# A planner's estimate of when transfers land and when GpSimd's queue slots come free, in a fused attention and MLP kernel on one core

## The chip, the core and the metric

The kernel runs on one core of a Trainium2 chip. The core has five engines that each work through a list of instructions in order: TensorE (PE in the profile, with its weight loads shown apart as PEld), VectorE (DVE), ScalarE (ACT), GpSimd (POOL) and SyncE (SP). They wait for each other by semaphores. SP, ACT and POOL also issue transfers (DMAs) between HBM and SBUF. Times are microseconds on the device; the metric is the median of the runs.

## The reference

The first half is attention with a squared ReLU in place of the softmax; its result, laid out as tokens by model width, goes through a two-layer MLP with a squared ReLU.

```
# q, k, v: (8, 12, 448, 64) float32; w_in: (768, 2048); w_out: (2048, 768)
scores = (1 / sqrt(64)) * q @ k.transpose(0, 1, 3, 2)
attn   = maximum(scores, 0) ** 2 / 448
o      = attn @ v                                  # (8, 12, 448, 64)
x      = o.transpose(0, 2, 1, 3).reshape(3584, 768)
h      = x @ w_in
r      = maximum(h, 0)
out    = (r * r) @ w_out                           # (3584, 768) float32
```

## The kernel before

**Work.** A unit `n` is four heads of one batch: 3 units per batch, 24 in all, 7 rounds per unit. For a unit the kernel brings q and k in, turns them (by TensorE, L441 with the copy L444, for units 0 to 5; by a transposing transfer on SP, L457, from unit 6 on, after a cast on GpSimd, L421) and brings v in (L471, two transfers). For each round TensorE makes scores (L502) into one of two PSUM tiles `sp`; the ReLU goes to one of four tiles `rel`, on VectorE (L529) or ScalarE (L532); the square goes to one of eleven tiles `at`, on ScalarE (L536) or GpSimd (L538). The seven squares of a unit are multiplied by v in one burst (L567), copied to `xt` (L587, L589). The first batch is cut in two parts by columns (128 and 320 of 448), so that work can start before all has landed.

**The MLP.** The first product of a batch is L629 (for the first part of the first batch L678, turned back at L705), its square and mask are L618 on ScalarE and L613 on VectorE. The second product is L778 for the first tokens and else L843, where seven products stand for eight (a Strassen scheme): their inputs are sums on VectorE (L822, `comb`), differences of the weights (L804 on GpSimd, L807 on VectorE), and results are copied (L762, L764), closed (L855) and stored by SP (L724). `rest` (L744, GpSimd) packs the last 64 tokens of two batches.

**First transfers.** GpSimd issues q and k of units 1 to 5 (L387), v (L471), the four quarters of `w_in` (L476, called w_0 to w_3 here, 768 KB each as written) and the four of `w_out` (L481). Its queue has eight slots in a ring, each with its own semaphore: the ninth transfer waits until the first has landed. GpSimd waits for this in its instruction list, so all that stands behind waits too.

**What sets the order.** No engine's list is written out by hand. Every operation is given to a `Plan` with its possible engines, costs, inputs, buffers and a due time. `simulate` runs a list schedule: each engine takes the earliest-due operation that is ready (`pick`), and the order in which operations were taken is the order in which they are emitted. A transfer's end in it comes from `land`, which shares a rate of 400e3 bytes per us among queues that have something to move, and adds a constant. For GpSimd, `self.sent` holds the time at which each transfer's slot comes free, and `pick` gives it no transfer while eight are taken:

```
if len(alt) == 5 and eng == "POOL" and sum(x > now for x in self.sent) > 7:
    continue
```

Sixteen pairs of two thresholds (`PATIENCE`: how long TensorE may idle before a filler matmul, L988, is put in its list, in the first 45 us; `LEAD`: how far ScalarE must be booked before GpSimd takes a late square) are tried, each with up to six rounds of `land`, and the schedule that ends first in the plan is emitted. On the chip, engines only wait for data: the plan's times are gone, its orders stay. TensorE starts with 9 matmuls on zeros (L985).

Of the kernel before, what the change touches and what calls it, by code (L numbers as in the profile page):

```python
# [42 lines left out]
class Plan:  # L43
# [72 lines left out]
    def land(self):  # L116


        queues: dict = {}
        for op in sorted((op for op in self.ops if op.size), key=lambda op: op.start):  # L120
            queues.setdefault(op.engine, deque()).append([op.start + 1.3, op.size, op])
        now, idle = 0.0, set(queues)
        while queues:
            for name in idle & set(queues):
                if queues[name][0][0] <= now + 1e-9 and set(queues) - idle:
                    queues[name][0][0] = now + 2.3
                    idle.discard(name)
            live = [name for name in queues if queues[name][0][0] <= now + 1e-9]
            idle -= set(live)
            if not live:  # L130
                now = min(q[0][0] for q in queues.values())
                continue
            rate = 400e3 / len(live)
            step = min(queues[name][0][1] / rate for name in live)
            later = [q[0][0] - now for q in queues.values() if q[0][0] > now + 1e-9]
            step = min([step] + later)
            now += step
            for name in live:
                q = queues[name]
                q[0][1] -= rate * step  # L140
                if q[0][1] <= 1e-3:
                    op = q.popleft()[2]
                    self.landing[op.id] = now + (
                        1.4 if len(queues) > 1 or now > 12.0 else 0.9) + (
                        1.0 if q and q[0][2].size > op.size else 0.0)
                    if not q or q[0][0] > now + 1e-9:
                        idle.add(name)
            queues = {name: q for name, q in queues.items() if q}

    def simulate(self):  # L150
# [10 lines left out]
        while done < len(self.ops):  # L161
            if not events:
                raise RuntimeError("no operation can go on")
            now = heapq.heappop(events)
            while events and events[0] <= now + 1e-9:
                heapq.heappop(events)
            again = True
            while again:
                again = False
                for eng in ("PE", "ACT", "DVE", "POOL", "SP"):  # L170
                    if self.busy[eng] > now + 1e-9:
                        continue
                    got = None
                    if eng == "PE" and last is not None and last.glue is not None:
                        soon = self.soon(last.glue)
                        if now < soon <= now + 0.45:
                            heapq.heappush(events, soon)
                            continue
                        if soon <= now:
                            got = waiting.index((last.glue.due, last.glue.id, last.glue)), (  # L180
                                last.glue.alts[0])
                    got = got or self.pick(eng, now, waiting)
                    if got is None:
                        if eng == "PE" and now < self.fill_until:
                            idle = now if idle is None else idle
                            if now < idle + self.patience:
                                heapq.heappush(events, idle + self.patience + 1e-3)
                            else:
                                self.fill(now)
                                heapq.heappush(events, self.busy[eng])  # L190
                        continue
                    z, alt = got
                    op = waiting.pop(z)[2]
                    _, busy, took, emit, *rest = alt
                    begin = now
                    op.size = rest[0] if rest else 0
                    if eng == "PE":
                        last, idle = op, None
                        begin += self.SWITCH.get((mode, op.mode), 0.0)
                        mode = op.mode  # L200
                        if now < self.cold:
                            busy, took = busy * 1.6, took * 1.6
                    if len(rest) > 1 and self.busy["POOL"] > now:
                        wait = self.busy["POOL"] - now
                        busy, took = busy + wait, took + wait
                    op.engine, op.start = eng, begin
                    op.end = begin + took
                    self.busy[eng] = begin + busy
                    if op.size:
                        op.end = max(begin + 2.2 + op.size / 390e3, self.landing.get(op.id, 0.0))  # L210
                        if eng == "POOL":
                            self.sent += [op.end] * (2 if op.size == 458752 and took > 1.0 else 1)
                    if len(rest) > 1:
                        self.busy["POOL"] = max(self.busy["POOL"], self.busy[eng])
                    for b in op.bufs:
                        if b.tile is None:
                            slot = min(x for x in self.pools[b.pool] if x[0] <= now + 1e-9)
                            self.pools[b.pool].remove(slot)
                            b.tile, b.slot = slot[2], slot[1]
                    self.order.append(emit)  # L220
                    heapq.heappush(events, self.busy[eng])
                    seen = op.end + self.LAG[eng]
                    for b in op.bufs:
                        b.left -= 1
                        b.end = max(b.end, op.end + 0.07)
                        if not b.left:
                            self.pools[b.pool].append((b.end, b.slot, b.tile))
                            heapq.heappush(events, b.end)
                    for x in op.nexts:
                        x.wait -= 1  # L230
                        x.ready = max(x.ready, seen)
                        if not x.wait:
                            insort(waiting, (x.due, x.id, x))
                            heapq.heappush(events, x.ready)
                    done += 1
                    again = True
# [922 lines left out]
```

## Time and profile before

| | |
|---|---|
| median of 5 runs | 386.84 us (386.36 to 388.29) |
| the profiled execution | 388.29 us, the highest of the five; its span is 386.4 us, so 1.9 us lie around it |
| PE busy | 372.7 us, 96% of the span |
| ACT busy, DVE busy, POOL busy | 279.3, 265.4, 173.5 us |
| squares on ScalarE, whole rounds (L536) | 108, 952 ns each |
| squares on GpSimd, whole rounds (L538) | 39, 1683 ns each |
| filler matmuls (L988) | 24 |
| TensorE clock granted | 1.000 |

The span runs from the first to the last instruction. "Busy" leaves out waits; a busy PE of 96% says that what can be won on the other engines is won only where TensorE waits for them. A group's line gives source line, engine, operation, tile written and tiles read, count, busy time and mean, and then the idle time of the engine before it with what ended it.

### The profile page before, as it was taken

The numbers are of one execution on the slowest core, as the hardware profiler recorded it, in microseconds if no ns is written. First come the engines' busy times: TensorE is split into PE (matmuls) and PEld (weight loads), VectorE is DVE, ScalarE is ACT, GpSimd is POOL, SyncE is SP. The second block draws the span as 40 slices with busy tenths as digits, with TensorE's granted clock in tenths as the row PEclk, the third lists the DMA queues.
The fourth block names the chain that finished last, engine by engine and source line by source line (L and its number), as shares of the span: only waits on it lengthen the run. The fifth ranks groups of instructions, "written<-read, shape, count | busy, mean of one in ns | idle before, by whom it ended". The sixth has DMA issues, their size and how long they took to land.

```text
span 386.4 us, 8331 instructions
## 1 busy us (share of the span) xinstructions
PE 372.7 (96%) x3299; PEld 198.1 (51%) x3299; DVE 265.4 (69%) x386; ACT 279.3 (72%) x417; POOL 173.5 (45%) x171
## 2 busy tenths in 40 slices
PE   7788999999999999999899999999999999999995
PEld 3545665544555445544455455544455546555563
DVE  2776789776876678676996675676886676256731
ACT  4988999898867887689786787695986785244221
POOL 6986558297753764562434444542602431001000
PEclk9999999999999999999999999999999999999999
DMA  9999999987578755569577664773562002210243
GB/s 185 177 208 193 177 225 236 230 183 169 72 201 188 166 146 113 114 164 233 61 192 124 155 158 87 186 172 68 146 125 61 2 3 52 65 28 1 55 110 83
DMA packets 70215, 51.34 MB, mean 133 GB/s; under 512 B 36896, under 2 KB 70176, under 8 KB 70176
## 3 DMA queue, kind: packets, MB, share of 16 engines
q1 hardware_dynamic: 52384, 35.86, 38.8%
q0 software_dynamic: 16928, 14.09, 24.7%
q10 hardware_dynamic: 864, 0.85, 0.6%
q8 instruction: 26, 0.43, 0.5%
q14 instruction: 13, 0.11, 0.1%
HBM read 45.61 MB, written 11.01 MB: 147 GB/s over the span
## 4 chain that ended last, share of the span: by engine, by line
PE 83%; DMA 8%; POOL 3%; DVE 2%; ACT 2%; issue 1%; SPq 0%; POOLq 0%
PE mm L629 36%; PE mm L843 29%; PE sp L502 8%; PE mm L567 7%; DMA vs<-in_v_dram 4%; PE mm L778 2%; DMA g<-in_k_dram 2%; DMA qkt<-blk 2%; DVE comb L822 1%; POOL at L538 1%; POOL w L476 1%; POOL g L387 1%; DVE rel L529 1%; ACT g L618 1%; PE mm L441 0%
## 5 line engine op out<-in xcount | busy, mean ns | idle before, releaser
L629 PE MATMUL mm<-xt,w 128*128 128x448 f16 (+1 forms) x768 | 148.9, 347 | 0.0
L538 POOL TENSOR_TENSOR at<-rel 128x896 f16<-128x896 f32 (+1 forms) x48 | 76.9, 1605 | 94.3 <-ACT rel L532 62.6
L613 DVE SCALAR_TENSOR_TENSOR g<-mm,g 128x448 f16<-128x448 f32 (+1 forms) x128 | 76.6, 605 | 54.4 <-ACT g L618 54.3
L536 ACT ACTIVATE at<-rel 128x896 f16<-128x896 f32 (+1 forms) x120 | 109.1, 931 | 3.6 <-PE mm L567 2.4
L629 PEld LDWEIGHTS <-w 128*128 128x128 f16 x768 | 72.2, 98 | 70.6 <-issue 12.3
L529 DVE TENSOR_SCALAR rel<-sp 128x896 f32<-128x896 f32 (+2 forms) x87 | 91.4, 1054 | 20.9 <-PE sp L502 17.3
L618 ACT ACTIVATE g<-mm 128x448 f16<-128x448 f32 (+1 forms) x128 | 66.9, 529 | 39.3 <-PE mm L629 38.6
L532 ACT ACTIVATE rel<-sp 128x896 f32<-128x896 f32 (+2 forms) x87 | 77.1, 891 | 7.2 <-PE sp L502 6.2
L843 PEld LDWEIGHTS <-comb 128*128 128x128 f16 x416 | 39.5, 98 | 31.7 <-issue 3.2
L502 PE MATMUL sp<-qkt,qkt 64*64 64x448 f16 (+2 forms) x756 | 50.8, 338 | 1.8 <-DVE rel L529 0.9
L421 POOL CAST blk<-raw 128x896 f16<-128x896 f32 x36 | 37.2, 1043 | 32.7 <-issue 15.9
L762 ACT ACTIVATE part<-mm 128x384 f32<-128x384 f32 x41 | 20.1, 489 | 42.0 <-PE mm L843 39.4
L855 DVE SCALAR_TENSOR_TENSOR part<-mm,part 128x384 f32<-128x384 f32 x52 | 28.7, 554 | 23.1 <-ACT part L762 14.3
L843 PE MATMUL mm<-wt,comb 128*128 128x384 f16 x208 | 37.0, 327 | 1.5 <-DVE comb L822 1.4
L843 PE MATMUL mm<-w,comb 128*128 128x384 f16 x208 | 36.8, 327 | 0.0
L567 PE MATMUL mm<-at,vs 64*64 64x448 f16 (+1 forms) x672 | 35.5, 343 | 1.1 <-POOL at L538 1.1
L843 PEld LDWEIGHTS <-g 128*128 128x128 f16 x264 | 25.2, 98 | 18.7 <-issue 2.5
L471 POOL DMA_DIRECT2D vs<-in_v_dram x48 | 29.8, 630 | 5.7 <-DMA w<-in_moe_w_in_dram 3.1
L502 PEld LDWEIGHTS <-qkt 64*64 64x64 f16 x756 | 18.1, 105 | 27.8 <-issue 23.9
L744 POOL COPY rest<-g 128x1024 f16<-128x1024 f16 x8 | 9.8, 1228 | 49.0 <-DVE g L613 49.0
L843 PE MATMUL mm<-w,g 128*128 128x384 f16 x176 | 30.9, 327 | 0.0
L567 PEld LDWEIGHTS <-vs 64*64 64x64 f16 x756 | 22.3, 107 | 14.0 <-issue 4.0
(60 smaller groups left out, 214.7 us busy)
## 6 DMA issues: line engine op xcount, KB each, us to landing
out_dram<-part SPq DMA_DIRECT2D x108, 96.0 KB, 2.2
raw<-in_k_dram SPq DMA_DIRECT2D x18, 448.0 KB, 4.1
raw<-in_q_dram SPq DMA_DIRECT2D x18, 448.0 KB, 4.8
vs<-in_v_dram POOLq DMA_DIRECT2D x48, 112.0 KB, 4.4
w<-in_moe_w_in_dram POOLq DMA_DIRECT2D x4, 768.0 KB, 12.2
w<-in_moe_w_out_dram POOLq DMA_DIRECT2D x4, 768.0 KB, 13.3
g<-in_k_dram POOLq DMA_DIRECT2D x4, 224.0 KB, 11.7
g<-in_q_dram POOLq DMA_DIRECT2D x4, 224.0 KB, 10.6
```

The costliest lines, as they stand in the source:

```text
L421: return lambda: fn(blk.tile.rearrange("p t (f d) -> p f t d", f=2), tile_of().rearrange("p f (t d) -> p f t d", d=D))
L471: nc.gpsimd.dma_start(out=buf.tile[64 * r:64 * r + 64], in_=src[:, u, hs])
L502: nc.tensor.matmul(sp[64 * c:64 * c + 64, e, c0:c0 + w].rearrange("p (t c) -> p t c", c=TP), lhsT=kT[r, t, 64 * e:64 * e + 64], rhs=qT[r, ...
L529: dve(n, lambda: nc.vector.tensor_scalar(out=rel(), in0=sp.tile[:, :, 0:width], scalar1=0.0, scalar2=SK, op0=ALU.max, op1=ALU.mult)),
L532: act(n, lambda: nc.scalar.activation(out=rel(), in_=sp.tile[:, :, 0:width], func=AF.Relu, scale=SK))],
L536: act(n, lambda: nc.scalar.activation(out=dst(), in_=rel(), func=AF.Square)),
L538: lambda: nc.gpsimd.tensor_mul(dst(), rel(), rel()))],
L567: nc.tensor.matmul(banks[f].tile[64 * e:64 * e + 64, c0:c0 + w], lhsT=vs[r, e ^ c, t * D:(t + 1) * D], rhs=a[r, e, :], start=(t == 0), sto ...
L613: nc.vector.scalar_tensor_tensor(out=dst, in0=src, scalar=0.0, in1=dst, op0=ALU.is_gt, op1=ALU.mult)
L618: nc.scalar.activation(out=dst, in_=src, func=AF.Square)
L629: nc.tensor.matmul(bank.tile[:, c0:c0 + w], lhsT=w1[f // 4][:, m, f % 4 * P:(f % 4 + 1) * P], rhs=xts[b].tile[:, m, cols], start=(m == 0), ...
L843: nc.tensor.matmul(buf.tile[:, 0:HALF], lhsT=lhs()[:, j, :], rhs=w[:, j, :], start=(first and j == 0), stop=(j == NH - 1), skip_group_chec ...
```

## The change

Three numbers in the plan change. In `land`, a transfer lands 2.1 us after its last byte has moved instead of 1.4 us (while more than one queue is at work, or after 12 us), and a transfer that is followed by a larger one in its queue gets 0.6 us more instead of 1.0 us. So a transfer is planned 0.7 us later, or 0.3 us later where a larger one follows. In `simulate`, a slot of GpSimd's ring comes free 0.8 us after the planned landing instead of at it. No operation, cost or buffer changes; the plan is made anew, and the emitted orders differ.

```
                     self.landing[op.id] = now + (
-                        1.4 if len(queues) > 1 or now > 12.0 else 0.9) + (
-                        1.0 if q and q[0][2].size > op.size else 0.0)
+                        2.1 if len(queues) > 1 or now > 12.0 else 0.9) + (
+                        0.6 if q and q[0][2].size > op.size else 0.0)
...
                         if eng == "POOL":
-                            self.sent += [op.end] * (2 if op.size == 458752 and took > 1.0 else 1)
+                            self.sent += [op.end + 0.8] * (2 if op.size == 458752 and took > 1.0 else 1)
```

The operations of the built program can be counted on each engine. After the change there are 36 filler matmuls instead of 24; 55 whole-round squares on GpSimd instead of 39, and 92 on ScalarE instead of 108; one of two pieces of a weight difference goes from GpSimd (L804) to VectorE (L807); four copies go from VectorE (L764) to ScalarE (L762); and some of the first copies and casts change between VectorE and ScalarE.

## The prediction

> **What bounds the kernel now.** I read the page's first lines, then the busy times by stage, then TensorE's waits by stage, then the timeline where a wait stands.
>
> ```profile
> PE 372.7 (96%) x3299; PEld 198.1 (51%) x3299; DVE 265.4 (69%) x386; ACT 279.3 (72%) x417; POOL 173.5 (45%) x171
> ```
> ```profile
> 0.00:32.00 32.00, 26.07 (x431) 14.90 (x432) 20.34 (x31) 25.22 (x38) 23.61 (x35) 1.00 1.12 191
> 32.00:45.00 13.00, 11.58 (x187) 7.48 (x185) 8.69 (x16) 11.24 (x18) 12.15 (x13) 1.00 1.16 176
> 45.00:350.00 305.00, 303.01 (x2494) 157.23 (x2493) 218.39 (x312) 234.20 (x346) 136.17 (x123) 1.00 0.62 133
> ```
>
> The second block has stage, length, busy PE, PEld, DVE, ACT, POOL, clock, DMA share, GB/s. From 45 to 350 us TensorE idles 1.99 us in 305; before 45 it idles 7.35 us, and some of its busy time there is filler. So the end is set by when TensorE gets its first data, then by its own work, then by a few waits. TensorE's waits from 45 to 350, then two of those before 45:
>
> ```profile
> PE mm L843 <- DVE comb L822: 1.2, 1, 1.2
> PE sp L502 <- DMA qkt<-blk: 0.6, 1, 0.6
> ```
> ```profile
> PE mm L567 <- POOL at L538: 1.1, 1, 1.1
> PE mm L678 <- DMA w<-in_moe_w_in_dram: 1.1, 2, 0.9
> ```
>
> After the last L678 both programs give TensorE the same matmuls, in the same order but for five places, with 122 changes between dense and 64x64 tiles instead of 124. So the difference is (a) when that L678 starts, (b) these waits, (c) new ones.
>
> **The start, to 32 us.** The timeline (start, length, engine, line; in brackets idle time before it):
>
> ```profile
> 11.07 0.84 POOL L476 DMA_DIRECT2D w<-in_moe_w_in_dram  x1 [0.68 <-DMA g<-in_k_dram]
> 11.93 1.26 POOL L538 TENSOR_TENSOR at<-rel 128x640 f16<-128x640 f32 x1
> 23.87 1.46 PE L678 MATMUL mm<-w,xt 128*128 128x512 f16 x6 [0.89 <-DMA w<-in_moe_w_in_dram]
> 31.97 0.59 POOL L471 DMA_DIRECT2D vs<-in_v_dram  x1 [3.10 <-DMA w<-in_moe_w_in_dram]
> 36.49 1.27 POOL L538 TENSOR_TENSOR at<-rel 128x640 f16<-128x640 f32 x1
> 37.82 0.47 PE L567 MATMUL mm<-at,vs 64*64 64x320 f16 x8 [1.09 <-POOL at L538]
> ```
>
> w_0 goes out at 11.07, when its slot is free, and the square follows. The landings of w_0 to w_3 in the trace are 20.02, 23.83, 27.66, 31.43: 3.8 us apart, one behind the other, and the four L678 start at 20.17, 23.87, 27.71 and 31.64. TensorE follows the weights. The DMA share is 1.29 at 12 to 13 us, 1.00 and 0.98 in the next two, 1.24 from 20: before w_0 the DMA engines ran partly dry, so w_0's landing hangs on its issue.
>
> The change puts that square ahead of w_0, and with w_0 all that GpSimd has behind it: the other weights, units 3 to 5, v. When can it run? Its rel is VectorE's second, read from the L502 that started at 9.14 behind turns which wait for k of unit 1 (landed 8.37). Seven fillers instead of one stand before the first turns: six more at 0.11 (six in a row take 0.83 in the trace, the last one's own 0.28 included) move them from 5.17 to 5.82. ScalarE then makes both copies, 256 and 512 columns, instead of VectorE: and one of the fillers waits for the first copy, since it writes the bank that is being read; the first scores start at about 7.1 instead of 6.95. All this ends in the wait for 8.37, which stays; behind it stands one more filler, 0.11. So rel is done at 10.45 instead of 10.34, the square runs 10.5 to 11.75, and w_0 goes out there: +0.7. A gain is excluded, for at 11.07 the slot had only just come free. Bounds: 0, if the dry stretch was the transfer's own and not its late issue; +1.35, if the 0.65 of the first turns gets through. I take +0.7, the row of the square. w_1 to w_3 are issued right behind (13.13 to 15.66 before, 12.6 to 15.1 now) and stay 3.8 us apart; their GpSimd waits cost nothing more. The last L678 starts at 32.3. The copies to xt, which the first L678 also needs, ended at 20.23 before; half a microsecond on them hides behind w_0's landing at 20.7.
>
> The other fillers (36 less 24, 1.3 us in all) stand where TensorE waits for w_1 to w_3, so the wait hides them; uncovered they cost 0.11 each.
>
> **32 to 45 us.** Before, GpSimd is stuck behind w_3's slot to 31.97, then does two squares (2.47), two transfers (35.0 to 36.5), then the square that TensorE waits for: at 37.82, 1.09 us of named wait and 1.4 us against the usual pace. After, only two squares are left behind the stuck v, one before each of the transfers of k and q: v at 32.7 to 33.3, square to 34.55, transfer to 35.3, square to 36.6. TensorE's burst starts 0.67 later, at 36.3, reaches the last two squares at 37.1, and does not wait. L441 follows at about 37.4 instead of 38.21; its second half needs q of unit 4, which landed at 37.19 and now lands near 37.9, so half a microsecond of gain is lost. What is late next is the copies to xt, which come with the burst. I take -0.65 at 45 us: +0.7 - 1.4 and a little; bounds -1.1 and +0.4.
>
> **78 us.** A turning transfer stands on SP behind four stores, is issued at 72.09 and lands at 77.95:
>
> ```profile
> 78.09 0.38 PE L502 MATMUL sp<-qkt,qkt 64*64 64x448 f16 x4 [0.63 <-DMA qkt<-blk]
> ```
>
> After, 12 of the L629 stand between this L502 and the one before it (at about 75.4). SP's list is the same up to here. TensorE arrives at about 78.2, when it has landed. 0.7 gained, 0.2 paid for two more changes of tile (a change back and forth takes 0.17 to 0.2 in the trace): -0.5, bounds -0.7 and 0.
>
> **186 to 189 us.**
>
> ```profile
> 185.49 2.60 POOL L421 CAST blk<-raw 128x896 f16<-128x896 f32 x2
> 187.23 1.41 DVE L822 TENSOR_TENSOR comb<-comb,g 128x1024 f16<-128x1024 f16 x1
> 188.69 1.47 PE L843 MATMUL mm<-wt,comb 128*128 128x384 f16 x8 [1.19 <-DVE comb L822]
> ```
>
> The sums of VectorE take 1.25 to 1.41 beside GpSimd's copies and casts, where undisturbed ones take 0.68. TensorE goes through two products at once and then waits for the second sum. After, an L502 pair (0.43) and a product without a sum (1.3) come between, 1.73 us of cover for 1.33 of wait (0.14 at 186.03, 1.19 here). I take -1.3; bounds -1.35 and 0, if GpSimd's three squares and its later rest copy hold VectorE up by as much again.
>
> **After that** the lists differ at 257 to 276 with four changes of tile fewer: -0.35 (bounds -0.4 and 0). The 16 squares moved take 15.2 us (16 x 0.952) from ScalarE and put 26.9 (16 x 1.683) on GpSimd; POOL is busy 136 of 305 there, so it has room, and ScalarE was no bound: 0 either way while the squares are done before their burst, which comes two pairs of L502, some 8 us, after the last scores. The end (last matmul, close, store) is the same list.
>
> **New waits.** Orders made with planned durations meet real ones. Before shows 2.0 us of such waits in three places after 45 us; for the new list I take a third, +0.7; bounds 0 and 4.
>
> For these last the nearest row is a square beside a sum:
>
> ```profile
> 240.54 1.68 POOL L538 TENSOR_TENSOR at<-rel 128x896 f16<-128x896 f32 x1 [1.19 <-ACT rel L532]
> 241.72 1.04 DVE L822 TENSOR_TENSOR comb<-comb,g 128x1024 f16<-128x1024 f16 x1
> ```
>
> The sum took 0.36 us more with 0.5 of the square left to run. The Trainium skill (SBUF — State Buffer, section "Who interferes with whom") speaks against the change here: a VectorE instruction with two SBUF inputs and a GpSimd one that reads SBUF block each other, the later waiting until the first is done. By that rule a sum that comes just behind a square's start loses up to the whole 1.68; three windows so hit would cost an estimated 3 x 1.68 = 5.0.
>
> **Sum.** -0.65 - 0.5 - 1.3 - 0.35 + 0.7 = -2.1. The span goes from 386.4 to 384.3. The profiled execution was the highest run (388.29); I put the same difference on the median, 386.84: 384.7.
>
> **Rivals.**
> *Given back* (0.20): the start costs the whole 1.35 instead of 0.7, and the sums of 188 us stay half as late; -2.1 + 0.65 + 0.65 = -0.8, so 386.0. For it: w_0 now waits for a chain of five engines' steps. Against: that chain meets at the landing of 8.37.
> *GpSimd in the way* (0.20): seven more windows like 186 us exist, where sums (L822) run; with more squares there, sums or the rest copy come late and TensorE waits 1.33 each. From the third window on it outweighs all: -2.8 + 3 x 1.33 = +1.2, so 388.0. For it: the rows above. Against: GpSimd would still be free for nearly half of the time (136 + 27 busy of 305), the long sums at 186 stand beside casts, whose number is unchanged, and beside a square a sum lost 0.36.
> *The orders differ but nothing that TensorE waits for does*: the three waits would have to stay; the lists at all three have changed. It is part of the first rival.
>
> **How the numbers follow.** 384.7 at 0.60. Without new waits and with the start at its better bound the sum is -2.8 - 0.45 = -3.25; the lowest run before lies 0.5 under its median, so the range begins at 383.1. The forecast's own range ends at 386.0, with new waits of 2.0. The whole range goes on over the first rival to 387.8, shortly before the second. About 0.3%, 1.2 us, is what a measurement of this kernel can tell from no change: the forecast lies beyond it on the fast side (0.60), the first rival within (0.20), the second beyond on the slow side (0.20).
>
> **What would show it.** Right: w_0 issued near 11.75 and landing near 20.7; the last L678 near 32.3; no wait of L567 for L538 near 37; no wait at L502 near 78; none at L843 near 186. Wrong: L678 past 33, or TensorE's idle time from 45 to 350 us above 3.

## The result, and the profile after

The changed kernel takes 385.52 us, median of 36 runs; the kernel before, run beside it, 387.42, median of 63. The ratio is 0.996 (95% interval 0.9948 to 0.9971), so the change makes it faster by 1.5 us (1.1 to 2.0) by the ratio and 1.9 by the medians. The prediction had a difference of -2.1 and 384.7; the kernel before came out 0.6 above the 386.84 that it was reckoned from.

The profiled execution took 385.16 us, its span is 383.4. That is 3.0 below the span before, more than the medians differ: the profile before was taken of a run 0.87 above the median of those 63, this one lies 0.36 below its own. The pair of profiles shows where time went; its total has 1.2 us of luck in it. One of the profiles further on (six fillers fewer) lies 6.6 us above its kernel's median; only its start and one wait are read.

The page of the changed kernel, then its busy times by stage (stage, length, busy PE, PEld, DVE, ACT, POOL, clock, DMA share, GB/s):

```profile
PE 374.7 (98%) x3311; PEld 200.5 (52%) x3311; DVE 267.5 (70%) x383; ACT 269.6 (70%) x407; POOL 194.3 (51%) x184
```
```profile
0.00:32.00 32.00, 28.62 (x442) 16.62 (x443) 20.45 (x32) 24.84 (x39) 22.97 (x33) 1.00 1.11 189
32.00:45.00 13.00, 12.70 (x194) 8.30 (x192) 10.01 (x17) 12.58 (x20) 11.04 (x13) 1.00 1.25 194
45.00:350.00 305.00, 304.39 (x2503) 158.64 (x2502) 220.60 (x310) 225.22 (x336) 158.76 (x138) 1.00 0.60 132
```

From 45 to 350 us TensorE idles 0.61 us (1.99 before). GpSimd is busy 22.6 us longer there, ScalarE 9.0 shorter, and VectorE 2.2 longer although it has two instructions fewer; the reason for the last number is given in the part on why the prediction was right. TensorE's waits, over the whole span (us in total, times, longest):

```profile
PE mm L678 <- DMA w<-in_moe_w_in_dram: 0.9, 1, 0.9
PE sp L502 <- DVE rel L529: 0.8, 3, 0.5
PE mm L567 <- ACT comb L536: 0.4, 2, 0.2
PE mm L843 <- DVE comb L822: 0.2, 1, 0.2
```

All three named waits of before are gone: L567 for L538 at 37 us, L502 for the transposing transfer at 78, L843 for a sum (1.2) at 188. A new one is in the second line. The timeline at the places that the prediction went through:

```profile
5.01 1.70 PE L988 MATMUL mm<-part 128*128 128x256 f16 x7
10.83 1.25 POOL L538 TENSOR_TENSOR at<-rel 128x640 f16<-128x640 f32 x1 [1.11 <-DVE rel L529]
12.03 3.36 POOL L476 DMA_DIRECT2D w<-in_moe_w_in_dram  x4
31.85 1.46 PE L678 MATMUL mm<-w,xt 128*128 128x512 f16 x6
36.10 1.15 PE L567 MATMUL mm<-at,vs 64*64 64x320 f16 x28
70.28 0.57 PE L502 MATMUL sp<-qkt,qkt 64*64 64x448 f16 x8 [0.48 <-DVE rel L529]
184.64 0.57 PE L502 MATMUL sp<-qkt,qkt 64*64 64x448 f16 x8
185.14 1.47 PE L843 MATMUL mm<-wt,g 128*128 128x384 f16 x8
185.29 2.33 DVE L822 TENSOR_TENSOR comb<-comb,g 128x1024 f16<-128x1024 f16 x1
186.45 2.76 PE L843 MATMUL mm<-wt,comb 128*128 128x384 f16 x16
```

The square is ahead of w_0, the burst (L567) runs through 28 matmuls without a stop, and at 185 us a pair of L502 and a product that reads no sum stand ahead of two products that run without a gap, although the second one's sum took 2.33 us. The starts of five matmuls that both programs have, and what each stage gained:

| start of | before | after | gain in the stage | predicted |
|---|---|---|---|---|
| the last L678 | 31.64 | 31.85 | +0.21 | +0.7 |
| the first L629 | 39.62 | 38.58 | -1.25 | -1.35 |
| the first L843 | 100.14 | 98.98 | -0.13 | -0.5, new waits +0.7 |
| the 400th L629 | 207.79 | 205.17 | -1.46 | -1.3 |
| the last matmul | 381.83 | 378.82 | -0.39 | -0.35 |

(The "400th" is that with 400 ahead of it, and so on.)

### The profile page after: what moved, and what is told of

It reads as the page before. It is cut to its first block, busy times and chain, and to the rows that moved or that the text cites. A ratio compares the mean times of both kernels' runs of the same rounds, so it can differ in the third digit from the quotient of the medians.

```text
span 383.4 us, 8363 instructions
## 1 busy us (share of the span) xinstructions
PE 374.7 (98%) x3311; PEld 200.5 (52%) x3311; DVE 267.5 (70%) x383; ACT 269.6 (70%) x407; POOL 194.3 (51%) x184
## 4 chain that ended last, share of the span: by engine, by line
PE 88%; DVE 5%; DMA 3%; ACT 2%; issue 1%; POOL 1%; DVEq 0%
PE mm L629 37%; PE mm L843 29%; PE sp L502 9%; PE mm L567 7%; DMA w<-in_moe_w_in_dram 3%; DVE comb L822 1%; DVE rel L529 1%; DVE wt L807 1%; PE mm L678 1%; PE mm L988 1%; PE mm L985 1%; ACT at L536 1%; PE mm L441 1%; PE mm L778 1%; ACT rel L532 0%
## 5 line engine op out<-in xcount | busy, mean ns | idle before, releaser
L629 PE MATMUL mm<-xt,w 128*128 128x448 f16 (+1 forms) x768 | 149.2, 347 | 0.0
L538 POOL TENSOR_TENSOR at<-rel 128x896 f16<-128x896 f32 (+1 forms) x63 | 102.4, 1626 | 90.2 <-ACT rel L532 57.9
L613 DVE SCALAR_TENSOR_TENSOR g<-mm,g 128x448 f16<-128x448 f32 (+1 forms) x128 | 76.5, 605 | 50.4 <-ACT g L618 50.2
L629 PEld LDWEIGHTS <-w 128*128 128x128 f16 x768 | 72.1, 98 | 70.2 <-issue 12.1
L529 DVE TENSOR_SCALAR rel<-sp 128x896 f32<-128x896 f32 (+3 forms) x87 | 90.7, 1046 | 22.4 <-PE sp L502 18.5
L536 ACT ACTIVATE at<-rel 128x896 f16<-128x896 f32 (+1 forms) x105 | 95.4, 926 | 4.8 <-PE mm L567 2.5
L618 ACT ACTIVATE g<-mm 128x448 f16<-128x448 f32 (+1 forms) x128 | 67.0, 529 | 45.0 <-PE mm L629 44.4
L532 ACT ACTIVATE rel<-sp 128x896 f32<-128x896 f32 (+1 forms) x87 | 77.6, 898 | 6.2 <-PE sp L502 5.1
L843 PEld LDWEIGHTS <-comb 128*128 128x128 f16 x416 | 39.8, 98 | 30.1 <-issue 3.5
L762 ACT ACTIVATE part<-mm 128x384 f32<-128x384 f32 x45 | 22.0, 488 | 44.0 <-PE mm L843 42.1
L502 PE MATMUL sp<-qkt,qkt 64*64 64x448 f16 (+2 forms) x756 | 51.2, 338 | 1.3 <-DVE rel L529 0.8
L421 POOL CAST blk<-raw 128x896 f16<-128x896 f32 x36 | 36.1, 1012 | 23.6 <-DMA raw<-in_k_dram 14.6
L843 PE MATMUL mm<-wt,comb 128*128 128x384 f16 x208 | 37.0, 327 | 0.2 <-DVE comb L822 0.2
L843 PE MATMUL mm<-w,comb 128*128 128x384 f16 x208 | 36.8, 327 | 0.1
L567 PE MATMUL mm<-at,vs 64*64 64x448 f16 (+1 forms) x672 | 35.3, 343 | 0.0
L843 PEld LDWEIGHTS <-g 128*128 128x128 f16 x264 | 25.2, 98 | 19.0 <-issue 2.7
L502 PEld LDWEIGHTS <-qkt 64*64 64x64 f16 x756 | 18.3, 105 | 27.1 <-issue 23.2
L471 POOL DMA_DIRECT2D vs<-in_v_dram x48 | 29.9, 633 | 3.9 <-DMA w<-in_moe_w_in_dram 2.1
L843 PE MATMUL mm<-w,g 128*128 128x384 f16 x176 | 30.9, 327 | 0.0
L567 PEld LDWEIGHTS <-vs 64*64 64x64 f16 x756 | 22.5, 107 | 12.1 <-issue 2.2
```

Source lines behind the costliest of these rows:

```text
L421: return lambda: fn(blk.tile.rearrange("p t (f d) -> p f t d", f=2), tile_of().rearrange("p f (t d) -> p f t d", d=D))
L471: nc.gpsimd.dma_start(out=buf.tile[64 * r:64 * r + 64], in_=src[:, u, hs])
L502: nc.tensor.matmul(sp[64 * c:64 * c + 64, e, c0:c0 + w].rearrange("p (t c) -> p t c", c=TP), lhsT=kT[r, t, 64 * e:64 * e + 64], rhs=qT[r, ...
L529: dve(n, lambda: nc.vector.tensor_scalar(out=rel(), in0=sp.tile[:, :, 0:width], scalar1=0.0, scalar2=SK, op0=ALU.max, op1=ALU.mult)),
L532: act(n, lambda: nc.scalar.activation(out=rel(), in_=sp.tile[:, :, 0:width], func=AF.Relu, scale=SK))],
L536: act(n, lambda: nc.scalar.activation(out=dst(), in_=rel(), func=AF.Square)),
```

## The experiments

The theory: TensorE gains where the new order ends a wait (37, 78, 186 us), and pays for a later w_0 and a few new waits; what else moves is beside the path. The rivals: the later planned landings or slots themselves make the gain; the squares taken off ScalarE make it; or it is luck of the start. Three kernels carry parts of the change, one is the changed kernel again, and the others edit the emitted order of one program at one place. For these the plan keeps the operation with each emission, and `ahead(a, b)` puts operation a's emission just before b's.

All in one table: the median, that of the kernel before in the runs beside it, the ratio of the two kernels with its 95% interval, and two stages of the profile. The medians of the kernel before differ by up to 0.7 us between these sets of runs, so kernels of different sets are compared by their ratios. "Start" is the last L678's start; "rest" goes from the first L629 to the start of the last matmul.

| kernel | median, us | before, beside it | ratio | start | rest |
|---|---|---|---|---|---|
| before (as profiled) | 386.84 | | | 31.64 | 342.21 |
| after (as profiled) | 385.52 | 387.42 | 0.996 (0.9948 to 0.9971) | 31.85 | 340.23 |
| after again | 385.43 | 387.50 | 0.9939 (0.9915 to 0.9963) | 31.96 | 340.83 |
| after, w_0 first | 384.94 | 387.50 | 0.994 (0.991 to 0.9969) | 30.86 | 340.00 |
| after, six fillers fewer | 385.62 | 387.50 | 0.995 (0.9928 to 0.9971) | 32.75 | not read |
| after, product back at 186 | 386.42 | 388.13 | 0.9973 (0.9948 to 0.9997) | 32.81 | 341.08 |
| after, one square back | 384.65 | 388.13 | 0.9907 (0.9879 to 0.9934) | 33.45 | 339.42 |
| after, all squares back | 389.14 | 388.06 | 1.0044 (1.0018 to 1.007) | 31.03 | 345.20 |
| before, loads behind the square | 387.46 | 388.13 | 0.9988 (0.9968 to 1.0009) | 32.32 | 343.51 |
| before, the new squares | 392.02 | 388.13 | 1.0103 (1.0077 to 1.0128) | 30.80 | 347.11 |
| 0.6 for 1.0 alone | 386.96 | 387.50 | 0.998 (0.9953 to 1.0006) | 30.75 | 343.15 |
| 2.1 and 0.6 alone | 388.79 | 388.06 | 1.0033 (1.0008 to 1.0057) | 31.89 | 343.01 |
| 0.8 on the slots alone | 388.13 | 388.06 | 1.0012 (0.9997 to 1.0028) | 31.18 | 342.41 |
| after, w_0 first and one square back | 384.01 | 387.75 | 0.9901 (0.9878 to 0.9924) | 30.77 | 340.16 |

**The changed kernel again.**

> The changed kernel once more, unaltered, for a second profile of it. Theory (three places where TensorE waited are repaired by the new order: a square at 37 us, a transfer at 78, a sum at 186): the waits of L567 for L538, of L502 for the transposing transfer and of L843 for a long sum are absent again, idle time of TensorE from 45 to 350 us is 0.6 +- 0.3 us, the time is 0.995 to 0.997 of the kernel before. Rival (luck at the start: the slowest DMA engine happened to be 0.3 us quicker with the last quarter of w_in): the last L678 starts at 32.1 to 32.4 instead of 31.85, the first L629 at 39.0 or later instead of 38.58, and the places after it look as before.

The ratio, 0.9939, lies a little below the range that was expected. The same three waits are gone, TensorE's idle time from 45 to 350 us is 0.98 (305 less 304.02, a little over the expected 0.9, with 0.92 at 70 us), the first L629 starts at 38.72. The start did not differ between these two profiles, but it does in others of this order: 32.75, 32.81 and 33.45, up to 1.6 us later. In the last two the weights are only a part of it: w_3 had landed 0.9 and 1.1 us before (31.92, 32.33), and TensorE came late from a stretch at half clock, shown at the end of this document. So one pair of profiles can't weigh the start; the "rest" column can be compared within about 0.6, which is what these two differ by.

**w_0 first.** In the changed kernel:

```
+        ahead(16, 67)     # L476 for w_0, the first GpSimd square
```

> The changed kernel with one instruction moved: w_0 (L476) is put ahead of the GpSimd square that the change set before it; every other list is the same. The prediction charged this square with +0.7 us. If that step holds, w_0 goes out at about 11.1 us instead of 12.03, the four quarters land 0.7 to 0.9 earlier, the last L678 starts at 31.0 to 31.2 instead of 31.85 and the run is 0.5 to 0.8 us shorter than the changed kernel (0.994 of the kernel before). Rival 1 (the DMA engines run dry before w_0 for another reason): the landings move by less than 0.3 and the time by nothing. Rival 2 (the square, now at 12 us, holds up the first burst, or GpSimd waits longer for the slot): gain at L678, lost again by the first L629 at 38.6.

```profile
10.22 0.84 POOL L476 DMA_DIRECT2D w<-in_moe_w_in_dram  x1 [0.56 <-DMA g<-in_k_dram]
11.08 1.26 POOL L538 TENSOR_TENSOR at<-rel 128x640 f16<-128x640 f32 x1
```

GpSimd's timeline: w_0 goes out when its slot comes free, the square follows at once and makes no one late (the rest is 340.00). The slot came free at 10.22 here, not 11.07. Over all profiles, w_0 is issued at 9.89 to 11.17 in the six with w_0 first (mean 10.44), and at 10.69 to 12.03 in the eight with the square first (mean 11.31): 0.87 later. w_3 lands at 31.00 and 31.81 in the mean, 0.81 later, and the last L678 starts at 31.19 and 32.12, 0.93 later. This is about the prediction's +0.7, seen only over many profiles, whose ranges overlap. The time, 0.5 below the changed kernel by the medians, is not told from it by the intervals.

**Six fillers fewer.** In the changed kernel, the first six L988 are not emitted.

> The changed kernel without six of the seven filler matmuls (L988) that stand before the first turns (L441). In the profile they took 0.21 us each, not the 0.11 of the prediction, so the first turns come 1.27 earlier, at 5.2 us. Theory: the first square on GpSimd is then ready at 10.5 instead of 10.83, w_0 goes out at 11.75 instead of 12.03, and the last L678 gains 0.3 us; the time 0.0 to 0.3 below the changed kernel. Rival (k of unit 1 at 8.4 us is what the start waits for, whatever comes before): nothing changes from 9 us on, 0.0. Rival (the fillers are what brings TensorE to its full pace): the first turns and scores take longer and the run is up to 0.5 us longer.

w_0 goes out at 11.31 instead of 12.03, and the time is that of the changed kernel. But three profiles with all seven fillers have w_0 at 11.33, 10.92 and 10.69: in these the fillers were quick. The timeline of the kernel with one square back, to be read against the 5.01 line of the changed kernel above:

```profile
1.20 3.64 PE L985 MATMUL mm<-part 128*128 128x512 f16 x9 [1.20 <-DVE part L982]
4.68 0.93 PE L988 MATMUL mm<-part 128*128 128x256 f16 x7
5.44 0.50 PE L441 MATMUL mm<-ident,blk 128*128 128x128 f16 x6
```

Seven fillers take 0.76 us here (5.44 less 4.68, 0.11 each), and 1.49 in the changed kernel's profile (6.50 less 5.01, 0.21 each). What the fillers cost is thus below what a run differs from the next; inconclusive.

**The product back at 186.** In the changed kernel:

```
+        ahead(874, 870)     # wt x g: behind both products that read sums
```

> The changed kernel with one product moved on TensorE: at 185 us the eight L843 on wt and g, which read no sum, go behind the two products that read sums; the pair of L502 stays ahead of them. The prediction gave the removed wait of 1.3 us to this cover. Theory: the long sum (2.33 us, done at 187.6) is then waited for again, by 0.9 to 1.3 us; the stretch from the 300th to the 400th L629 grows from 44.97 to about 46.1 us, the time by about 1.1, and all else stays. Rival (the gain of 1.46 there came from the sums or the tile changes, not from the cover): the stretch stays within 0.3 us of 44.97.

```profile
186.00 1.47 PE L843 MATMUL mm<-wt,comb 128*128 128x384 f16 x8
188.55 1.48 PE L843 MATMUL mm<-wt,comb 128*128 128x384 f16 x8 [1.07 <-DVE comb L822]
189.86 1.46 PE L843 MATMUL mm<-wt,g 128*128 128x384 f16 x8
```

The wait is back with 1.07 us, and the stretch from the 300th to the 400th L629 takes 45.92 against 44.97. That is clear of the spread: with the cover in place the stretch takes 44.96 or 44.97 in all six profiles of this order that keep the new squares, or all but one of them. So the cover makes two thirds of the 1.46 that this stage gained; the L502 pair that stayed is the likely rest. The time can't tell it: the ratio, 0.9973, lies above both of the changed kernel's, but the intervals overlap.

**Loads behind the square.** In the kernel before:

```
+        ahead(80, 82)     # k of unit 5, now behind the square (157)
+        ahead(81, 82)     # q of unit 5
```

> The kernel before with two loads moved on GpSimd: k and q of unit 5 (L387) go behind the square that TensorE waited for at 37 us instead of ahead of it; all else as before. Theory: the square runs at 35.0 instead of 36.5, the wait of L567 for L538 (1.1 us) is gone, the first L629 starts at 38.4 to 38.7 instead of 39.62, and the run is 1.0 us shorter than the kernel before. Rival (what comes next, the turns of unit 4, is held by its transfers or by the copies to xt): the wait is gone and another takes its place, and the first L629 gains less than 0.3.

```profile
36.68 1.12 PE L567 MATMUL mm<-at,vs 64*64 64x320 f16 x28
71.32 0.38 PE L502 MATMUL sp<-qkt,qkt 64*64 64x448 f16 x4 [0.56 <-DVE rel L529]
78.89 0.38 PE L502 MATMUL sp<-qkt,qkt 64*64 64x448 f16 x4 [1.29 <-DMA qkt<-blk]
```

The burst does not stop, and from the last L678 to the first L629 it takes 6.82 us instead of 7.98. But the wait at 78 us has grown from 0.63 to 1.29, one at 71 appears, and from the first L629 to the 100th it takes 36.47 instead of 35.84, to the first L843 61.81 instead of 60.52. The time is the kernel before's within the interval. What was won at 37 us was given back by 100, a part of it where a transfer sets the time; neither expectation had that. In the changed kernel 12 L629 stand in front of that transfer's reader, and no wait is seen there.

**The new squares alone.** In the kernel before, 31 squares change their engine, none its place:

```
+        moved = {248, 319, 353, ...}
+        for y, (z, eng, emit) in enumerate(order):
+            if z in moved:
+                emit = next(a[3] for a in self.ops[z].alts if a[0] != eng)
+                order[y] = z, eng, emit
```

> The kernel before with the engines of the changed kernel for the whole-round squares behind 45 us: 23 go from ScalarE to GpSimd and 8 the other way, each at its old place in the emitted order; TensorE's, VectorE's and SP's lists are the kernel's before. Theory of the prediction (ScalarE was no bound, squares are done before their burst): 0, within 0.4 us of the kernel before; the waits of L502 at 78 and of L843 at 188 stay. Rival 1 (relieving ScalarE is where the change gains): 1 to 2 us shorter. Rival 2 (GpSimd in the way: the runs showed two-input instructions of VectorE that took 2 to 5.9 us beside GpSimd's squares and differences, against 0.7 to 0.95 alone): 0.5 to 2 us longer, with waits of TensorE for sums (L822) or for VectorE's ReLU (L529) that the kernel before has not.

It takes 1.0% longer, 4.0 us: the way of Rival 2, at twice its size. First its waits, then the timeline:

```profile
PE mm L843 <- DVE comb L822: 3.0, 3, 2.1
PE sp L502 <- DVE rel L529: 2.4, 5, 1.2
```
```profile
184.55 1.68 POOL L538 TENSOR_TENSOR at<-rel 128x896 f16<-128x896 f32 x1
184.94 1.84 DVE L822 TENSOR_TENSOR comb<-g 128x1024 f16<-128x1024 f16 x1
186.70 3.10 DVE L822 TENSOR_TENSOR comb<-g,g 128x1024 f16<-128x1024 f16 x1
186.17 1.26 POOL L471 DMA_DIRECT2D vs<-in_v_dram  x2
187.41 1.84 POOL L421 CAST blk<-raw 128x896 f16<-128x896 f32 x2
190.46 2.39 PE L843 MATMUL mm<-wt,comb 128*128 128x384 f16 x8 [2.15 <-DVE comb L822]
```

The first sum ends at 186.78, 0.55 after the square (186.23); the second at 189.80, 0.55 after the casts (189.25). A sum alone takes 0.68: these two did nearly all their work after GpSimd had finished. In the kernel before, two sums met one cast each here and took 1.41; now the second sum has both casts to wait for. It starts 0.71 before the first of them, while GpSimd issues transfers (L471); why it doesn't end before them is open.

Not all that this kernel loses is such waiting. The waits of L843 for sums have grown from 1.4 to 3.0 us. Behind the longest TensorE's matmuls take up to twice as long until 194.3 (2.39 us for eight that take 1.47), an estimated 1.6 us in all from these and the next 24; the clock granted there is 0.50. And at 277 three squares stand in a row on GpSimd (270.95 to 275.91): a ReLU on ScalarE waits 1.45 for them, the square and mask of L629's result come late behind it, and L629 waits 1.02. No sum or difference of VectorE is in that path.

**0.6 instead of 1.0, alone.** In `land`:

```
-                        1.0 if q and q[0][2].size > op.size else 0.0)
+                        0.6 if q and q[0][2].size > op.size else 0.0)
```

> One third of the change alone: 0.6 instead of 1.0 us for a transfer that is followed by a larger one; the other two numbers as before. Its list has w_0 ahead of the first GpSimd square as before, no filler before the first turns, two loads and not one ahead of the square that TensorE waited for at 37 us (one square fewer is in that queue too), the L843 of 186 us covered as in the changed kernel, the L502 of 78 us not covered, and 55 squares on GpSimd like the changed kernel. Theory (the places count, not the numbers): -0.9 at 37 us, 0 at 78, -1.4 at 186, up to +0.7 of new waits: 1.6 to 2.3 us below the kernel before, about the changed kernel's time. Rival (it is the later planned landing and slot that make the gain): within 0.5 us of the kernel before.

The first L629 starts at 37.26, and the stretch from the 300th to the 400th L629 takes 44.95: both places gain as the theory has it. But from the first to the 300th it takes 124.54 (121.75 before), 2.8 us of new waits where 0.7 was allowed for. The largest:

```profile
74.49 5.86 DVE L807 TENSOR_TENSOR w<-w,w 128x1536 f16<-128x1536 f16 x1
74.76 1.71 POOL L538 TENSOR_TENSOR at<-rel 128x896 f16<-128x896 f32 x1
76.41 3.12 POOL L804 TENSOR_TENSOR w<-w,w 128x1536 f16<-128x1536 f16 x1
```
```profile
PE mm L629 <- DVE g L613: 1.3, 1, 1.3
```

A weight difference that takes 0.95 alone took 5.86, through a square and a difference of GpSimd, and the mask behind it (L613) let TensorE wait 1.3. The changed kernel has the same instructions; there two transfers are issued between GpSimd's square (74.31) and its difference (77.20), and VectorE's difference, from 75.0 on, ended 0.81 after the square: 1.81. So the theory of places held in the stages and its price for new waits did not. The time (0.998, with 1 inside the interval) is not the 1.6 to 2.3 us less that it had, and does not exclude the rival.

**The landing alone, the slot alone.** In `land` both constants, or in `simulate` the 0.8.

> The two constants of the landing alone (2.1 instead of 1.4 us; 0.6 instead of 1.0), the slot free at the landing as before. Its list: w_0 behind the first GpSimd square as in the changed kernel; at 37 us two loads stand ahead of the awaited square, and one square fewer before them; L502 of 78 us and L843 of 186 us not covered; 26 whole-round squares on GpSimd (39 before, 55 in the changed kernel), 19 fillers. Theory (the places count): the start costs 0.7, the wait at 37 us shrinks by about 0.5, the waits at 78 and at 186 to 189 us (1.0 and 1.3) stay, so 0.998 to 1.001 of the kernel before. Rival (a later planned landing makes the gain): 0.994 to 0.997.

> The third number alone: GpSimd's slots come free 0.8 us after the planned landing; landings as before. Its list: w_0 behind the first GpSimd square; at 37 us one load and not two ahead of the awaited square; nothing changed at 78 and 186 us; 39 whole-round squares on GpSimd as before, 24 fillers. Theory: the start costs 0.7, the wait at 37 shrinks by 0.7 but what is won there is waited for again at 71 to 78 us, where a transfer sets the time (as in the kernel with two loads moved), so 0.999 to 1.002 of the kernel before. Rival (the slot's time makes the gain): 0.994 to 0.997.

Neither gains. The rivals that put the gain on the numbers fall: with the landing the run is slower by 0.3% (a little more than the theory had), with the slot the same. Both profiles still have L843 waiting for L822 by 1.2, as before, and from the 300th to the 400th L629 46.21 and 46.44. With the landing alone, GpSimd has 13 squares fewer, and L502 waits 1.6 for L529 and 0.7 for L532. The gain belongs to the one order that all three numbers happen to give.

**One square back.** In the changed kernel, the square of 63.4 us goes to ScalarE:

```
+            if z == 319:
+                order[y] = z, "ACT", self.ops[z].alts[0][3]
```

The changed kernel's timeline shows why it was chosen (the L502 that waits is the 70.28 line shown above):

```profile
63.40 1.68 POOL L538 TENSOR_TENSOR at<-rel 128x896 f16<-128x896 f32 x1
63.80 3.69 DVE L807 TENSOR_TENSOR wt<-w,wt 128x1536 f16<-128x1536 f16 x2
65.02 1.65 POOL L421 CAST blk<-raw 128x896 f16<-128x896 f32 x1
69.15 1.08 DVE L529 TENSOR_SCALAR rel<-sp 128x896 f32<-128x896 f32 x1
```

> The changed kernel with one square given back: the one that the change moved to GpSimd at 63.4 us runs on ScalarE, at its place in the order. In the changed kernel's profile two weight differences (L807) start on VectorE at 63.8 beside this square and the cast behind it and take 3.69 us instead of 1.9; VectorE's ReLU comes behind them, and L502 waits for it at 70.28 (0.65 us above its usual pace, 0.92 in the second profile). Theory (that new wait is the square's doing): the two differences take 0.7 to 1.1 us less and the wait at 70 is 0 to 0.2; the run 0.5 to 0.9 shorter than the changed kernel. Rival (the cast alone holds VectorE up as much, or the differences wait for w_out): the wait stays above 0.4. Rival (ScalarE is then late with its own ReLU, 0.95 us later): a wait of L502 for L532 takes its place.

```profile
65.73 2.58 DVE L807 TENSOR_TENSOR wt<-w,wt 128x1536 f16<-128x1536 f16 x2 [0.24 <-DMA w<-in_moe_w_out_dram]
```

The pair takes 1.11 us less, no wait is left at 70, and the rest is 339.42, 0.8 to 1.4 below the two profiles of the changed kernel. The kernel with w_0 first and the one with the product back keep the square, and the wait (0.39 and 0.50). So in this order the new wait was the square's doing, though a cast can do as much: with all squares back, in the next run, 0.39 us of a wait for L529 stand there, behind a difference beside a cast.

**All squares back.** In the changed kernel the same 31 squares get their old engines.

> The changed kernel with the engines of the kernel before for the whole-round squares behind 45 us: 23 go back from GpSimd to ScalarE, 8 from ScalarE to GpSimd, each at its place in the emitted order; TensorE's, VectorE's and SP's lists are the changed kernel's. The same move the other way in the kernel before cost 1.0%. Theory (squares on GpSimd only cost, by holding up VectorE's two-input instructions, and the new order of TensorE covers most of it): the long sum at 185 us falls from 2.33 to 1.4 and the wait at 70 us (0.65 to 0.92) goes, with nothing new: 0.4 to 0.8 us below the changed kernel, 0.992 to 0.995 of the kernel before. Rival (the new order is made for a ScalarE with 15 fewer squares; with them back its ReLUs and squares come late): new waits of TensorE for L532 or L536, 0.5 to 3 us longer than the changed kernel.

It is slower than both kernels: 389.14, ratio 1.0044. Two of its waits, then the timeline at the largest and at the one for L613:

```profile
PE sp L502 <- ACT rel L532: 1.8, 3, 1.4
PE mm L567 <- DVE g L613: 0.9, 2, 0.7
```
```profile
73.67 3.13 POOL L804 TENSOR_TENSOR w<-w,w 128x1536 f16<-128x1536 f16 x1
74.10 3.75 DVE L807 TENSOR_TENSOR w<-w,w 128x1536 f16<-128x1536 f16 x1
78.89 0.95 ACT L536 ACTIVATE at<-rel 128x896 f16<-128x896 f32 x1 [1.37 <-DVE rel L529]
79.75 0.90 ACT L532 ACTIVATE rel<-sp 128x896 f32<-128x896 f32 x1
80.70 0.38 PE L502 MATMUL sp<-qkt,qkt 64*64 64x448 f16 x4 [1.41 <-ACT rel L532]
225.52 1.79 ACT L536 ACTIVATE at<-rel 128x896 f16<-128x896 f32 x2
228.45 1.51 PE L567 MATMUL mm<-at,vs 64*64 64x448 f16 x27 [0.74 <-DVE g L613]
```

At 79 us a square stands ahead of the ReLU on ScalarE, waits 1.37 for its own input, and TensorE waits for the ReLU. But this square stands there in the changed kernel too (at 77.84). What is new is that its input is late, behind a difference on VectorE that took 3.75, and GpSimd's own difference is what it met. In the changed kernel a square keeps GpSimd busy first, so that the two differences miss each other:

```profile
74.31 1.68 POOL L538 TENSOR_TENSOR at<-rel 128x896 f16<-128x896 f32 x1
77.20 3.13 POOL L804 TENSOR_TENSOR w<-w,w 128x1536 f16<-128x1536 f16 x1
```

With that square back on ScalarE, GpSimd's difference starts at 73.67 and meets VectorE's. The profile with six fillers fewer, where no square went back, has the same meeting (VectorE's takes 4.29) and the same wait of 1.41 behind it. So the largest wait does not show a ScalarE with too much to do. The one at 228 does: two squares in a row on ScalarE hold up its L618 of the MLP, VectorE's mask (L613) comes late behind that, and TensorE waits for VectorE. Matmul by matmul against the changed kernel's profile, 1.9 us of delay arise at 79 us, 0.9 between 110 and 116, behind sums beside a square that went to GpSimd, and 1.7 from 225 us on, behind ScalarE. The rival was right in its sign, and its reason (the new order is made for a ScalarE with 15 squares fewer) holds for a part; one square could go back at a gain.

**Both moves.** w_0 first, and the one square back.

> The changed kernel with the two moves together: w_0 ahead of the first GpSimd square, and the square of 63.4 us back on ScalarE. Theory (independent places): w_0 goes out 0.7 to 1.1 us earlier than in the changed kernel's profiles with this order (10.7 to 12.0), so at 9.9 to 11.1; no wait of TensorE at 70 us; from the first L629 to the last matmul 339.3 to 339.6 us (340.2 and 340.8 in the changed kernel's two profiles, 339.4 with the square back alone); time 0.990 to 0.993 of the kernel before. Rival (what is won at the start is waited for again at 70 to 80 us, where transfers set the time): the stretch grows above 340.2 and the time stays at 0.994.

w_0 goes out at 10.13, TensorE's excess at 70 us is 0.17, but one of 0.37 appears at 78.5, and the rest is 340.16: a part is given back, between theory and rival. The median is 384.01, ratio 0.9901 (0.9878 to 0.9924): faster than the kernel before, and than the changed kernel's 0.996 (0.9948 to 0.9971); against its second measurement, 0.9939 (0.9915 to 0.9963), the intervals overlap by a little. From the kernel with the square back alone (0.9907) it is not told: what w_0 adds is not resolved in the time.

## Why the prediction was right, point by point

**The sum.** -2.1 was predicted, the medians say -1.9, the ratio -1.5. In the pair of profiles (see the table of stages) three terms hold within 0.2 us: those of 37, 186 and 257 us. The start shows 0.5 less than its term, and the stage with the 78 us place and the new waits 0.3 less than the two together, so the pair's total is -3.0, of which some 1.2 lie in which runs were profiled.

**The start, +0.7.** That the square ahead of w_0 delays its issue is shown by moving w_0; that L678 follows is seen in the means (0.87 at the issue, 0.93 at L678), not in the time. The working was partly luck: fillers at 0.21 instead of 0.11 put the first turns at 6.50 where 5.82 was worked out, and the square came at 10.83 instead of 10.5, which the wait for k of unit 1 did not wholly absorb. In the pair of profiles only 0.21 of it is seen at L678, since the slowest DMA engine lagged less for the last weights: 1.4 us behind the first one (30.36 to 31.77), against 1.9 before. The prediction had w_0 landing 9 us after its issue, near 20.7; it landed at 19.62, earlier than before, and at 20.51 in the second profile.

**37 us, -1.4.** -1.25 in the pair. The prediction added this to later terms as if TensorE kept what it had gained. The move of the loads alone showed that it does not while the transfer at 78 us is uncovered.

**78 us, -0.5.** The wait is gone, with a new one of 0.65 at 70 us in the same stage. That the 12 L629 in front of it are what covers it is read from the order; no run took them away. The term "new waits, +0.7" was met in size by that wait, which is luck: its cause, one moved square beside VectorE's differences, was only found afterwards.

**186 us, -1.3.** -1.46; the cover is shown by taking it away (0.95). It was nearly used up: the prediction feared that the sum could come later by as much again, and 2.33 instead of 1.41 came true.

**257 to 276 us, -0.35.** -0.39 in that stage of the pair; only read, no run took it alone.

**Squares, 0 either way.** This is the step whose reason failed. "It has room", said of GpSimd, is wrong for the old order: 15 more squares there cost 4.0 us. "ScalarE was no bound" is wrong in part for the new one: with 15 squares brought back the kernel is 3.3 us longer by the ratios (1.0044 against 0.996), and in the profile 1.7 us of delay stand behind ScalarE, 1.9 behind the meeting of two differences. The net of zero came out for the new order as a whole, in which matmuls and squares moved together; that this is why, is argued and not shown. The price of the rival *GpSimd in the way* (some 4 us of waits) was near the 4.0 of the squares alone, but by luck: only 1.6 us of those are more waiting for sums. Its chance was argued from the wrong row: the 0.36 us that one sum lost beside the end of a square is the mild case; the same class of instruction lost 0.7 to 4.9 in these runs. VectorE's sums and differences behind 45 us took 48.5 us before and 53.4 after (one instruction more, 0.95); the other 4 us are such losses, of which TensorE saw about 0.65. In the squares-only kernel they took 54.4 with the count of before, and TensorE saw more of it.

The rule cited in the prediction, from the Trainium skill (SBUF — State Buffer, section "Who interferes with whom"), that a VectorE instruction with two SBUF inputs and a GpSimd one block each other, agrees with these rows in that VectorE's ends 0.55 behind the end of a square and of a cast. It has the later one wait; here VectorE's difference at 74.49 started before GpSimd's square (74.76), and the sum at 186.70 before the casts (187.41), and yet both waited. That one instruction must wait for more than one of GpSimd's in a row (5.86 us, through a square and a difference) is what these runs add to the weight of it. The estimate of 5.0 us for three such windows is not met by the squares alone, where the waits for sums grew by 1.6.

## What to carry to other kernels

Price an engine's instruction by whom it blocks, not by how idle the engine is: look in the trace for the longest row of each kind beside a neighbour's work, and give that its share of the range. A gain ahead of a wait whose end is set by a transfer is kept only if that wait is covered as well, so terms along the path may not simply be added. Where a scheduler makes the order, judge the order and not the number that was turned: three constants whose parts showed no gain clear of the noise gave one together, and one square moved back by hand on that order took the ratio from 0.996 to 0.9907 (with w_0 first as well, 0.9901).

## What the runs showed of the hardware

- VectorE's sum of two fp16 tiles (0.68 us alone) or difference (0.95) takes up to 3.25 and 5.86 us beside GpSimd's squares, casts and differences. The sums read here end 0.55 after GpSimd's instruction, the differences 0.82 (80.35 after 79.53) and 1.05 (77.85 after 76.80).
- TensorE's first matmuls run at half pace for a time that differs from run to run: seven fillers took 0.11 us each in one profile from 4.68 us on, 0.21 in another from 5.01 on, with the same program up to there.
- The 16 DMA engines don't finish a transfer together, and how far they are apart differs between runs: for w_3, 1.4 us (30.36 to 31.77) in the changed kernel's profile and 2.7 (29.59 to 32.33) in that with one square back.
- A long wait costs TensorE more than itself. In all profiles here, its waits of 1.70, 1.71, 2.12 and 2.15 us within the kernel were each followed by 3.4 us at a granted clock of 0.50, and none of up to 1.44 us was. Once more half clock stands without one such wait (16.2 to 19.6 us with 0.6 for 1.0 alone). Two of the four are waits for w_0, and two for VectorE. With one square back w_0's engines were 3.1 us apart; the first L678 and the stretch behind it (stage, length, busy PE, PEld, DVE, ACT, POOL, clock, DMA share, GB/s):

```profile
21.26 2.62 PE L678 MATMUL mm<-w,xt 128*128 128x512 f16 x6 [1.70 <-DMA w<-in_moe_w_in_dram]
21.50:24.50 3.00, 3.00 (x18) 1.12 (x20) 0.08 (x1) 0.58 (x1) 0.77 (x1) 0.50 1.25 207
```

These six L678 take 1.46 at full clock. So a late weight moves the start of the last L678 twice: by its lag, and by the matmuls at half pace behind the wait.
